# A capped attention with a token-mixing feed-forward layer on one Trainium2 core: the first load in one piece, the cap behind it, and fewer, larger products of zeros at the start

## The chip, the core and the metric

The kernel runs on one core of a Trainium2 chip. The metric is the device time of one execution in microseconds; the time of a kernel is the median of its runs. A profiled execution is a run of its own, with its own time.

## What is computed

The inputs are q, k and v for 4 batches of 12 heads, 448 tokens and a head dimension of 64, all in fp32, and four matrices of a feed-forward layer. In short:

```
scores = q k^T / 8                      (per batch and head, 448 x 448)
scores = cap * tanh(scores / cap)       (cap is an input, 30.0)
attn   = softmax(scores);  x = attn v   (heads side by side: 448 x 768 per batch)
h      = (x^T U V)^T                    (mixing over tokens, rank 32)
u      = x + h
out    = u + relu(u w_ch1) w_ch2        (768 -> 3072 -> 768)
```

## The kernel before

All arrays are held transposed, with features on the partitions. Attention works on pairs of heads: one tile `qk` of 128 x 2 x 448 words (448 KB) holds q and k of two heads, 64 partitions each. `four` lays out the work of four such pairs: `scores` (L435) multiplies one block of 128 keys of both heads with all queries, one head on the lower 64 rows of the array and one on the upper; `tanh` (L440, on ScalarE) reads the scores from PSUM with the scale `qsc` = 1/(8 cap); `exp` (L450, on ScalarE) follows for two blocks at once with the scale `capt` = cap. `rest` (L464) and `full` (L476) multiply with v; `normalize` and `mixin` do the softmax division (its reciprocals go through DRAM and come back as `rb`, L539) and the token mixing. The feed-forward layer follows: `up_seven` (L765) and `down` (L823), whose weights are converted by VectorE and ScalarE during the attention.

No order of instructions is written out by hand. Every step is a task with estimated costs per engine, an extra delay `lat` for loads, a priority (a smaller number goes first) and a due time `begin` in ns, before which it is not ready. `simulate` plays the tasks through with these estimates and so fixes the order of instructions on each engine; `emit` writes them out in that order. On the chip each engine then works through its own list and waits where an operand isn't there. So an estimate or a due time moves nothing directly; it can change the order. The PSUM tile of a first block of a step and that of its second (`sc`, `sc2`) must both be free before the next two blocks begin. The plan puts a task on TensorE only when nothing of lower number is ready, and charges 210 ns where its `mode` differs from that of the task before.

Three places are touched by the change.

- `consts` (L302 to 314) runs ahead of everything: it issues the load of the cap on ScalarE's queue as 128 words of 4 bytes, fills the tile `ones`, and computes `qsc` on VectorE (L313, L314).
- `fill` (L357 to 369) puts 25 products of zeros on TensorE, each 64 rows by 128 columns with 192 columns of data. Each fp32 product appears in the trace as two matmul records. The first 9 are due from 1000 ns every 330 ns with the first priority of all, the other 16 from 4000 ns every 600 ns with the last priority.
- In `four` the first `qk` tile is loaded by two DMAs (L408): all of q with the first 128 keys (288 KB), and the other 320 keys (160 KB). All other `qk` and `vn` (v) tiles come in one DMA each. All go through SP's queue. The planner charges each `qk` load of the first four pairs 2 ns a column of SP's time, so 1792 for a whole tile.

Of the kernel before, what the change touches and what calls it, by code (L numbers as in the profile page):

```python
# [11 lines left out]
F32 = mybir.dt.float32  # L12
# [3 lines left out]
AF = mybir.ActivationFunctionType  # L16
ALU = mybir.AluOpType

B, H, S, D = 4, 12, 448, 64
# [13 lines left out]
EARLY = 5, 6, 3, 2, 7, 1, 4  # L33

ALONE = 12
FILL, FIRST = 25, 9

# [206 lines left out]
class Build(Plan):  # L246
# [54 lines left out]
    def consts(self):  # L301
        nc = self.nc  # L302
        pool = self.opened(self.cp)
        self.capt = pool.tile([128, 1], F32, name="capt")
        nc.scalar.dma_start(out=self.capt, in_=self.cap.broadcast_to((128, 1)))
        self.qsc = pool.tile([128, 1], F32, name="qsc")
        self.ident = pool.tile([128, 128], F32, name="ident")
        self.ones = pool.tile([128, 3, 32], F32, name="ones")
        nc.vector.memset(self.ones, 0.0)
        nc.vector.memset(self.ones[:, 0], 1.0)  # L310
        for i in range(2):
            nc.vector.memset(self.ones[64 * i:64 * i + 64, 1 + i], 1.0)
        nc.vector.reciprocal(self.qsc, self.capt)  # L313
        nc.vector.tensor_scalar(out=self.qsc, in0=self.qsc, scalar1=1.0 / D ** 0.5, scalar2=None, op0=ALU.mult)  # L314

# [37 lines left out]
    def fill(self):  # L353


        nc = self.nc
        z = self.buf("ta", [128, DM // 2], F32, self.wp)  # L357
        bank = self.psum("misc")

        def blank(e):  # L360
            e.memset(z.t, 0.0)

        def turn():
            nc.tensor.matmul(bank.t[:, :192], z.t[:64, :128], z.t[:64, 192:], start=True, stop=True)  # L364

        self.task({"POOL": 500}, blank, w=[(z, 0)], prio=-1000)
        for i in range(FILL):
            begin = 1000 + 330 * i if i < FIRST else 4000 + 600 * (i - FIRST)
            self.task({"PE": 330}, turn, r=[(z, 0)], w=[(bank, 0)], begin=begin, prio=-1000 if i < FIRST else 1000, mode="sc")

    def attention(self):
# [17 lines left out]
    def four(self, p):  # L389


        nc = self.nc
        pools = (self.ap, self.pre) if p < ALONE else (self.ap,)
        prios = [p + i // 2 * 2 - 100 for i in range(4)]
        qks, vns = [], []
        for i in range(4):
            b, q = divmod(p + i, NP)
            if i % 2 == 0:
                vn = self.buf("vn", [128, 7, 2, D], F32, self.ap)
                vns.append(vn)  # L400
            qk = self.buf("qk", [128, 2, S], F32, *pools)
            qks.append(qk)

            cuts = (0, S + 128, 2 * S) if p + i == 0 else (0, 2 * S)
            for n, (lo, hi) in enumerate(zip(cuts, cuts[1:])):

                def load(b=b, q=q, qk=qk, lo=lo, hi=hi):
                    nc.sync.dma_start(  # L408
                        out=qk.t.rearrange("p a s -> p (a s)")[:, lo:hi],
                        in_=self.qk[b, q].rearrange("p a s -> p (a s)")[:, lo:hi])  # L410

                self.task({"SP": 2 * (hi - lo) if p == 0 else 350}, load,
                    w=[(qk, n), *([(qk, 1)] if len(cuts) == 2 else [])], lat=2600 if p == 0 else 4200, prio=prios[i])
            if i % 2:
                self.task({"SP": 350}, lambda b=b, q=q, vn=vn: nc.sync.dma_start(out=vn.t, in_=self.v[b, q // 2]),
                    w=[(vn, 0)], lat=4000, prio=prios[i], begin=6000 if p == 0 else 0)
# [3 lines left out]
        for g in range(7):  # L420
            th = self.buf("th", [128, 2, 2, S], F32, *pools)
            pss = [self.psum("sc", 2), self.psum("sc2", 2)]
            prio = prios[steps[2 * g][0]]
            for j in range(2):
                i, t = steps[2 * g + j]
                where[i, t] = th, j
                ps = pss[j]
                cs = (i - 1, i) if t == 3 else (i,)

                def scores(i=i, t=t, ps=ps, cs=cs):  # L430
                    for c in cs:
                        out = slice(64 * (c % 2), 64 * (c % 2) + 64) if t == 3 else slice(0, 128)
                        for a in range(2):
                            hd = slice(64 * a, 64 * a + 64)
                            nc.tensor.matmul(  # L435
                                ps.t[out, a, :S], qks[c].t[hd, 1, 128 * t:min(S, 128 * t + 128)], qks[c].t[hd, 0],
                                start=True, stop=True)

                def tanh(j=j, ps=ps, th=th):
                    nc.scalar.activation(out=th.t[:, j], in_=ps.t[:, :, :S], func=AF.Tanh, scale=self.qsc)  # L440

                r = [(qks[c], k) for c in cs for k in range(1 + (t > 0))]
                if j == 0:
                    self.task({"PE": 750}, scores, r=r, w=[(ps, 0), (pss[1], "next")], prio=prio, mode="q" if t == 3 else "sc")
                else:
                    self.task({"PE": 750}, scores, r=[*r, (pss[1], "next")], w=[(ps, 0)], prio=-300, mode="q" if t == 3 else "sc")
                self.task({"ACT": 920}, tanh, r=[(ps, 0)], w=[(th, j)], prio=prio)

            def exp(th=th):
                nc.scalar.activation(out=th.t, in_=th.t, func=AF.Exp, scale=self.capt)  # L450

            ks = [(th, 0), (th, 1)]
            self.task({"ACT": 1790}, exp, r=ks, w=ks, prio=prio)

        for h in range(2):
            vn, prio, i0 = vns[h], prios[2 * h], 2 * h
# [11 lines left out]
            for i, o in enumerate(os):  # L468
# [12 lines left out]
                def add(e, in0, in1, out):  # L481
# [5 lines left out]
                    prio=prio, lock=True)  # L487
                self.task({"DVE": 1090}, partial(add, in0=whole, in1=at(ts[2]), out=whole), r=ts[2:], w=[(es, 0)],
                    prio=prio, lock=True)
                if p < ALONE:  # L490
# [3 lines left out]
                        r=[(rth, rj)], w=[(es, 0)], prio=prio, lock=True)  # L494
                b, q = divmod(p + i0 + i, NP)
                u = self.u_bufs[b]
                self.task({"DVE": 620, "ACT": 560}, lambda e, q=q, o=o, u=u: self.copy(e, u.t[:, q], o.t[:, :S]), r=[(o, 0)],
                    w=[(u, q)], prio=prio)
# [405 lines left out]
```

## Time and profile before

| | us |
|---|---|
| three runs | 894.3, 893.38, 893.54 |
| median | 893.54 |
| the profiled execution | 890.19 |
| its span, from the first to the last instruction | 888.4 |
| TensorE busy in it | 874.8 (98%) |
| ScalarE busy | 447.1 (50%) |
| VectorE busy | 656.0 (74%) |
| first tanh of scores starts at | 8.88 |

Engines in the profile: PE is TensorE's matmul, PEld its weight loads, DVE VectorE, ACT ScalarE, POOL GpSimd, SP SyncE; a q behind the name is the engine's sequencer or its DMA issues. A group line gives engine, operation, output<-input, shapes, count and durations. The profile's rows of granted clock (PEclk) begin with the first recorded change; what the clock was before is to be read from the durations of like instructions.

### The profile page before, as it was taken

What the parts mean: (1) busy time and instruction counts of PE and PEld (TensorE: products, weight loads), DVE (VectorE), ACT (ScalarE), POOL (GpSimd) and SP (SyncE); (2) the same over time, 40 slices, a digit from 0 to 9 for tenths busy, and PEclk for the clock granted to TensorE, in tenths of its full rate; (3) what the DMA queues carried; (4) which work ended last, traced back from release to release, by engine and by line L of the source; (5) the groups of instructions that cost most, each with busy time, mean ns of one, the idle gap of its engine ahead of it and who ended that gap; (6) DMA issues with size and microseconds to landing.
All of it is one profiled execution on the core that took longest, in us unless ns stands there. A gap on an engine that the chain in (4) does not pass through costs nothing.

```text
span 888.4 us, 11752 instructions
## 1 busy us (share of the span) xinstructions
PE 874.8 (98%) x4418; PEld 701.3 (79%) x4418; DVE 656.0 (74%) x1116; ACT 447.1 (50%) x649; POOL 91.8 (10%) x125
## 2 busy tenths in 40 slices
PE   9999999998999999999999999999999999999998
PEld 6334343345899999998999999999999999999997
DVE  2688888858887777876877898776777766777644
ACT  5989898986554454554565455332223221232210
POOL 0111111110122111121121112000000000000000
PEclk9999999998999999999999999999999999999999
DMA  5653444412578887878978647521212212122003
GB/s 195 222 185 100 125 141 150 135 45 67 145 207 253 236 233 210 217 210 250 265 205 223 182 96 197 189 71 36 63 45 72 72 36 72 38 69 72 1 1 124
DMA packets 42424, 121.13 MB, mean 136 GB/s; under 512 B 5728, under 2 KB 18432, under 8 KB 42368
## 3 DMA queue, kind: packets, MB, share of 16 engines
q1 hardware_dynamic: 23024, 79.29, 28.0%
q0 software_dynamic: 12288, 22.22, 13.3%
q10 hardware_dynamic: 7056, 18.88, 5.4%
q8 instruction: 34, 0.56, 0.2%
q14 instruction: 22, 0.18, 0.1%
HBM read 79.28 MB, written 24.47 MB: 117 GB/s over the span
## 4 chain that ended last, share of the span: by engine, by line
PE 67%; issue 18%; POOL 4%; DVE 4%; ACT 3%; DMA 3%; POOLq 0%; ACTq 0%; DVEq 0%
PE mm L823 29%; PE mm L765 25%; PE sc L435 4%; PE o L476 4%; POOL u L836 4%; ACT th L440 2%; DMA rb<-rd 1%; PE misc L364 1%; PE misc L582 1%; DMA u<-st 1%; PE o L464 1%; ACT th L450 1%; PE misc L566 1%; DMA rd<-r 1%; DVE es L482 1%
## 5 line engine op out<-in xcount | busy, mean ns | idle before, releaser
L823 PE MATMUL mm<-g,w 128*128 128x448 f32 x1728 | 374.9, 366 | 1.3 <-ACT st L239 0.7
L823 PEld LDWEIGHTS mm<-g,w 128*128 128x128 f32 x1728 | 324.1, 188 | 30.9 <-ACT st L239 1.9
L765 PE MATMUL mm<-x,ws 128*128 128x448 f32 x1512 | 334.8, 369 | 2.8 <-DVE x L639 1.4
L765 PEld LDWEIGHTS mm<-x,ws 128*128 128x128 f32 x1512 | 285.3, 189 | 28.9 <-DVE x L639 1.7
L828 DVE TENSOR_TENSOR u<-u,mm 128x448 f32<-128x448 f32 x216 | 134.0, 621 | 58.2 <-PE mm L823 50.8
L239 ACT ACTIVATE cx<-mm 128x448 f32<-128x448 f32 x72 | 39.1, 545 | 118.4 <-PE mm L765 107.0
L836 POOL DMA_DIRECT2D u<-st x72 | 62.5, 868 | 265.7 <-ACT st L239 254.1
L778 DVE TENSOR_TENSOR cx<-cx,mm 128x448 f32<-128x448 f32 x72 | 44.6, 620 | 57.4 <-PE mm L765 56.8
L440 ACT ACTIVATE th<-sc,qsc 128x896 f32<-128x896 f32 x84 | 80.4, 1003 | 9.6 <-PE sc L435 9.5
L239 ACT ACTIVATE st<-mm 128x448 f32<-128x448 f32 x72 | 39.3, 546 | 86.5 <-PE mm L823 56.8
L435 PE MATMUL sc<-qk 64*128 64x448 f32 (+1 forms) x384 | 79.3, 574 | 0.6 <-ACT th L440 0.4
L450 ACT ACTIVATE th<-th,capt 128x1792 f32<-128x1792 f32 x42 | 75.3, 1793 | 1.1
L239 ACT ACTIVATE ws<-wa 128x384 fp32r<-128x384 f32 x53 | 27.2, 521 | 81.3 <-PE mm L765 81.2
L239 ACT ACTIVATE g<-cx 128x448 fp32r<-128x448 f32 x72 | 41.6, 578 | 42.6 <-DVE cx L778 40.3
L476 PE MATMUL o<-th,vn 128*64 128x448 f32 x288 | 60.2, 554 | 0.0
L639 DVE TENSOR_TENSOR ws<-ta,ws 128x384 fp32r<-128x384 f32 x96 | 53.0, 553 | 4.2 <-ACT ws L239 3.7
L292 DVE SCALAR_TENSOR_TENSOR wa<-wa,wr 128x768 int32<-128x768 int32 (+2 forms) x50 | 46.7, 935 | 11.8 <-ACT wa L284 11.0
L435 PEld LDWEIGHTS sc<-qk 64*128 64x128 f32 (+1 forms) x384 | 29.0, 175 | 31.5 <-issue 15.4
L482 DVE TENSOR_TENSOR es<-es,th 128x896 f32<-128x896 f32 (+1 forms) x36 | 39.1, 1086 | 13.8 <-ACT th L450 13.3
L695 DVE TENSOR_TENSOR w<-wa,w 128x768 fp32r<-128x768 f32 x48 | 45.7, 954 | 4.3 <-ACT w L239 4.1
L239 ACT ACTIVATE ws<-ta 128x384 fp32r<-128x384 f32 x58 | 30.2, 522 | 35.4 <-PE mm L765 32.2
L476 PEld LDWEIGHTS o<-th,vn 128*64 128x64 f32 x288 | 18.8, 138 | 36.6 <-issue 34.5
(67 smaller groups left out, 636.3 us busy)
## 6 DMA issues: line engine op xcount, KB each, us to landing
wr<-in_w SPq DMA_DIRECT2D x48, 768.0 KB, 5.6
kept<-wa ACTq DMA_DIRECT2D x48, 384.0 KB, 5.8
wa<-kept SPq DMA_DIRECT2D x48, 384.0 KB, 3.2
u<-st POOLq DMA_DIRECT2D x72, 224.0 KB, 5.3
qk<-in_qk SPq DMA_DIRECT2D x23, 448.0 KB, 3.8
vn<-in_v SPq DMA_DIRECT2D x12, 448.0 KB, 3.3
rb<-rd POOLq DMA_DIRECT2D x24, 224.0 KB, 3.7
out_t<-u SPq DMA_DIRECT2D x24, 224.0 KB, 2.9
```

Of the source, the lines that this page charges most:

```text
L239: e.activation(out=out, in_=in_, func=func)
L292: nc.vector.scalar_tensor_tensor(out=a_t().bitcast(I32), in0=a_t().bitcast(I32), scalar=3, in1=raw_t()[:, 0::2], op0=ALU.logical_shift_lef ...
L435: nc.tensor.matmul(ps.t[out, a, :S], qks[c].t[hd, 1, 128 * t:min(S, 128 * t + 128)], qks[c].t[hd, 0], start=True, stop=True)
L440: nc.scalar.activation(out=th.t[:, j], in_=ps.t[:, :, :S], func=AF.Tanh, scale=self.qsc)
L450: nc.scalar.activation(out=th.t, in_=th.t, func=AF.Exp, scale=self.capt)
L476: nc.tensor.matmul(o.t[64 * a:64 * a + 64, :S], vn.t[:, 3 * i + t, a], th.t[:, j, a], start=False, stop=t == 2)
L482: e.tensor_tensor(out=out(), in0=in0(), in1=in1(), op=ALU.add)
L639: e.tensor_tensor(out=lo, in0=src(), in1=hi.bitcast(F32), op=ALU.subtract)
L765: nc.tensor.matmul(ps.t[:, :S], ws[p].t[:, wi, sl], xs[p].t[:, xi, d], start=fresh and n == 0, stop=n == 8, skip_group_check=not fresh)
L823: nc.tensor.matmul(ps.t[:, :S], w1[f].t[:, wi, sl], g[b, f].t[:, gi], start=f == fs[0] and i == 0, stop=f == fs[-1] and i == 2)
L828: nc.vector.tensor_tensor(out=u.t[:, d], in0=u.t[:, d], in1=ps.t[:, :S], op=ALU.add)
L836: nc.gpsimd.dma_start(out=u.t[:, d], in_=st.t, accum_op=ALU.add)
```

## The change

The load of the cap moves from ScalarE's queue to SP's, right behind the first `qk` load, together with the two VectorE instructions that make `qsc` of it (`scales`). The first `qk` load becomes one DMA. ScalarE does a tanh of a column of `ones` at the beginning. The products of zeros use all 128 rows; there are 18 in place of 25, 5 of them first (due every 660 ns) and 13 from 7000 ns every 600 ns. The planner's estimate of a `qk` load of the first four pairs goes from 1792 ns (2600 later landed) to 900 ns (2900 later landed).

```diff
-FILL, FIRST = 25, 9
+FILL, FIRST = 18, 5
...
-        nc.scalar.dma_start(out=self.capt, in_=self.cap.broadcast_to((128, 1)))
...
+        warm = pool.tile([128, 1], F32, name="warm")
+        nc.scalar.activation(out=warm, in_=self.ones[:, 0, :1], func=AF.Tanh)
+
+    def scales(self):
+        nc = self.nc
+        nc.sync.dma_start(out=self.capt, in_=self.cap.broadcast_to((128, 1)))
         nc.vector.reciprocal(self.qsc, self.capt)
         nc.vector.tensor_scalar(out=self.qsc, in0=self.qsc, scalar1=1.0 / D ** 0.5, scalar2=None, op0=ALU.mult)
...
-            nc.tensor.matmul(bank.t[:, :192], z.t[:64, :128], z.t[:64, 192:], start=True, stop=True)
+            nc.tensor.matmul(bank.t[:, :192], z.t[:, :128], z.t[:, 192:], start=True, stop=True)
...
-            begin = 1000 + 330 * i if i < FIRST else 4000 + 600 * (i - FIRST)
+            begin = 1000 + 660 * i if i < FIRST else 7000 + 600 * (i - FIRST)
...
-            cuts = (0, S + 128, 2 * S) if p + i == 0 else (0, 2 * S)
-            for n, (lo, hi) in enumerate(zip(cuts, cuts[1:])):
-
-                def load(b=b, q=q, qk=qk, lo=lo, hi=hi):
-                    nc.sync.dma_start(
-                        out=qk.t.rearrange("p a s -> p (a s)")[:, lo:hi],
-                        in_=self.qk[b, q].rearrange("p a s -> p (a s)")[:, lo:hi])
-
-                self.task({"SP": 2 * (hi - lo) if p == 0 else 350}, load,
-                    w=[(qk, n), *([(qk, 1)] if len(cuts) == 2 else [])], lat=2600 if p == 0 else 4200, prio=prios[i])
+            def load(first=p + i == 0, b=b, q=q, qk=qk):
+                nc.sync.dma_start(out=qk.t, in_=self.qk[b, q])
+                if first:
+                    self.scales()
+
+            self.task({"SP": 900 if p == 0 else 350}, load, w=[(qk, 0)], lat=2900 if p == 0 else 4200, prio=prios[i])
...
-                r = [(qks[c], k) for c in cs for k in range(1 + (t > 0))]
+                r = [(qks[c], 0) for c in cs]
```

## Rows read from the trace of the kernel before

**Rows 1.** The page: the chain by engine; one kind of DMA issue with its median.
```profile
PE 67%; issue 18%; POOL 4%; DVE 4%; ACT 3%; DMA 3%; POOLq 0%; ACTq 0%; DVEq 0%
...
rb<-rd POOLq DMA_DIRECT2D x24, 224.0 KB, 3.7
```
**Rows 2.** The chain of waits, 0 to 40 us: start, length, what it was.
```profile
1.21 5.80 PE misc L364 x17
7.01 3.31 PE sc L435 x8
10.32 1.70 PE misc L364 x9
12.02 1.83 PE sc L435 x12
13.85 1.66 PE misc L364 x9
15.50 1.67 PE sc L435 x8
17.17 0.65 PE misc L364 x4
17.82 0.91 PE o L464 x8
18.73 2.40 PE o L476 x12
...
39.00 7.45 DMA rb<-rd
```
**Rows 3.** Timeline of ScalarE, first 16 us: start, length, [idle before <- releaser].
```profile
5.79 1.28 ACT L440 ACT_TABLE_LOAD   x1 [5.79 <-DVE qsc L314]
8.88 1.01 ACT L440 ACTIVATE th<-sc,qsc 128x896 f32<-128x896 f32 x1 [1.80 <-PE sc L435]
11.41 1.79 ACT L450 ACTIVATE th<-th,capt 128x1792 f32<-128x1792 f32 x1
15.03 1.79 ACT L450 ACTIVATE th<-th,capt 128x1792 f32<-128x1792 f32 x1
```
**Rows 4.** Zero products at 1.8 to 6.4, then 10.8 to 11.6; then scores, 6.9 to 10.2.
```profile
L364 PE MATMUL misc<-ta x16: 524/524/683, 1.2 to 6.2; 64*128 64x192 f32 x16
L364 PE MATMUL misc<-ta x7: 322/323/451, 10.4 to 11.5; 64*128 64x192 f32 x7
L435 PE MATMUL sc<-qk x8: 951/951/1112, 6.5 to 9.4; 64*128 64x448 f32 x8
```
**Rows 5.** DMA issues at 0.8 to 1.2, then at 22 to 23: KB, us to landing.
```profile
qk<-in_qk SPq DMA_DIRECT2D x1, 288.0 KB, 4.2
qk<-in_qk SPq DMA_DIRECT2D x1, 160.0 KB, 4.7
capt<-in_cap ACTq DMA_DIRECT2D x1, 0.5 KB, 4.6
...
qk<-in_qk SPq DMA_DIRECT2D x1, 448.0 KB, 3.1
```
**Rows 6.** One stretch; the last two columns are the DMA engines' busy share and GB/s.
```profile
2.00:4.00 2.00, 2.00 (x8) 2.00 (x8) 0.00 (x0) 0.00 (x0) 0.00 (x0) 1.00 0.66 127
```
**Rows 7.** Records of 448 columns at 60 to 100 us: 128 rows, then 64 rows.
```profile
L515 PE MATMUL misc<-es,ones x24: 539/551/563, 63.3 to 95.8; 128*32 128x448 f32 x24
L435 PE MATMUL sc<-qk x80: 536/536/640, 61.5 to 98.1; 64*128 64x448 f32 x64, 64*64 64x448 f32 x16
```
**Rows 8.** Two stretches in which TensorE starved; last columns: granted clock, DMA share, GB/s.
```profile
46.00:48.00 2.00, 0.31 (x3) 0.31 (x4) 1.46 (x2) 1.75 (x2) 0.20 (x1) 1.00 0.91 347
214.00:216.00 2.00, 0.47 (x1) 0.19 (x1) 2.00 (x5) 2.00 (x5) 0.00 (x0) 0.87 0.00 0
```
**Rows 9.** The chain of waits again, 34 to 110 us.
```profile
48.34 1.70 PE o L464 x8
50.04 3.21 PE o L476 x12
```

## The prediction

> **What bounds the kernel now.** I read the chain of waits by engine first, then the same chain in order of time. TensorE holds most of it [rows 1], so a microsecond that TensorE's list begins earlier is kept, unless something that doesn't move comes in between. The chain's first pieces are the place of the change [rows 2]: nine products of zeros (18 records, of which 17 are merged in the row) hold TensorE from 1.21 to 7.01, then come the first two blocks of scores up to 10.32, then five more zero products. The reader is to see that nothing but zeros stands on the chain until 7.01, although the first part of q/k had landed at 0.74 + 4.2 = 4.9 [rows 5]. ScalarE's timeline shows what waits: its table load from 5.79 to 7.07, idle 1.80 behind it for the scores, the first tanh at 8.88, the first exp at 11.41, the second at 15.03 [rows 3].
>
> The durations show the clock. A zero product takes 524 ns from 1.2 until past 6.2 and 323 from about 10.7 on; the first score records take 951, later ones 536 [rows 4, 7]. So up to some 10.5 us TensorE ran at 1.2 GHz, and at 2.4 after. It had been busy without a gap since 1.21, with products on 64 rows; the clock rose only after the first scores, which use both halves of the array.
>
> **The change part by part.** *Fewer zeros first.* Ten records stand ahead of the first scores instead of 18. The plan keeps that order, by its own estimates (used for the order alone): the fifth is due at 3640 and ends at 3970, the q/k tile is ready at 900 + 2900 = 3800, so the scores come sixth. At the low clock a record costs between 5.80/17 = 0.34 and (6.2 - 1.2)/15 = 0.33 [rows 2, 4], so 8 fewer are 2.6 us, and TensorE would be free for scores at 7.0 - 2.6 = 4.4. No row shows a zero product on 128 rows. The bounds are a 128-row and a 64-row record of 448 columns, 539 to 551 and 536 ns [rows 7]: rows cost next to nothing, 3% at most of 3.2 us, 0.1. I take 0.
>
> *The load.* In one piece it must land by 4.4. Alone on the DMA engines, a load of 448 KB takes 3.1 us from issue to landing [rows 5], so 0.74 + 3.1 = 3.85 is the early bound. The late bound is the second part of before, issued some 0.4 behind the first: 0.74 + 0.4 + 4.7 = 5.85. Between 2 and 4 us the DMA engines were busy 0.66 of the time for only 127 GB/s [rows 6], beside the cap's 128 words of 4 bytes, which landed at 0.74 + 4.6 = 5.3 from the other queue. With the cap behind it on the same queue, the load is nearest to the lone one; I take 4.1 (the first packets of a run may be late), which TensorE doesn't feel. At 5.85 the gain would fall by 1.45.
>
> *The cap* now lands behind 448 KB. VectorE's two instructions let ScalarE go 0.45 after its landing (5.79 - 5.34) [rows 3, 5]; VectorE has only these queued ahead of the first sum of exponentials, whose input is made after them anyway. The first tanh has its scores at 8.88 - 2.6 = 6.3, so the cap may land until 5.85. Early bound: with the load, 4.1. Late bound: its whole 4.6 counted from the load's landing, 8.7. I take 5.3, as before, since 16 engines then have 8 small words each and no rival. It costs nothing, with half a microsecond in hand. A page of the Trainium skill speaks against this move: by "DMA: Bandwidth & Descriptors" (Queues, rings and completion order), each engine takes descriptors in ring order, and a completion count lands only after every earlier write of that engine. By that the cap can't report before the whole q/k load has landed, where before it had its own ring. No run so far shows it; what it does here is a rival below.
>
> *The tanh of ones* brings the 1.28 us table load [rows 3] to the beginning, where ScalarE idles until 5.79. It saves nothing of before (1.80 idle stood behind the load), but without it the table would be ready at 5.75 + 1.28 = 7.0, 0.7 too late.
>
> *Queues.* SP issues as many DMAs ahead of the second q/k tile as before (the cap in place of the second part); ScalarE issues one less. The fifth q/k tile goes ahead of v in the new plan (SP is free at 3600, v is due at 6000). v is first used at 17.82 [rows 2], and all these loads are over by some 12. POOL's list stays.
>
> *The later zeros.* In the old plan five products follow the first two blocks, five the next two, two the next; the trace shows just these (records are halves) [rows 2]. By the new due times none fits the first gap, six go into the second, one into the third. Count from the start of the first exp, when both score tiles are free. Before: 12.02 - 11.41 = 0.61 of leftover zeros, 1.83 scores, 1.66 zeros, 1.67 scores, 0.65 zeros, so `rest` begins at 6.41. After: 1.83 + 1.98 + 1.67 + 0.33 = 5.81; the exp that `rest` needs ends at 15.03 + 1.79 - 11.41 = 5.41. So `rest` begins 0.6 sooner, and TensorE's chain with it [rows 2, 3]. If the old blocking stays, 0.
>
> *The clock.* If it doesn't rise before the second block of scores is done, the first exp comes at 11.41 - 2.6 = 8.8. If it is up when the first scores begin, tanh waits for the cap: two tanh of 1.01 from 5.75 give an exp at 7.8, 1.0 sooner. Full-array zeros followed by scores are what it rose after, so it should come some time within the scores; I take 0.3 of 0 to 1.0.
>
> Sum: 2.6 + 0.6 + 0.3 = 3.5 us. The profiled execution was 890.19 (span 888.4 and 1.8 around it) and would be 886.7. The median of the runs is 893.54, 3.35 above it, so I carry the gain over to that: 890.0.
>
> **Rivals.** *The clock rises during the zeros.* For it: full-array products with no gap. Against: 5.8 us of half-array zeros did nothing. The gain is 2.6 + 0.6 + 1.0 = 4.2: 889.3.
>
> *The cap becomes the bound*, behind 448 KB in one queue and with 128 reads of one word. At the late bound of 8.7 `qsc` is ready at 9.15, two tanh follow, the exp starts at 11.2: gain 0.2, and 0.6 later, so 892.7. It decides from a landing of 5.85, and in full only near 8.7. Against it: before, those words took less than that even in competition. The page named above points to this rival.
>
> *The gain doesn't arrive.* The two stretches in which TensorE starves, at 46 and 214 [rows 8], lie behind a read of `rb` [rows 2] and behind VectorE, busy 2.00 of 2.0 in the second. If these don't move with the start, 893.5. Against: their inputs are made by the same chain.
>
> *Slower: a new order.* Due times of 15000 and 20000 ns (the mixing constants, the first weights) stay, while the plan's attention moves up by 210 to 420 ns, so tasks after some 20 us of plan can change places. The place with a price is the `rb` read: 7.45 us on the chain among weight and q/k loads [rows 2], median 3.7 [rows 1]. TensorE starved for it (0.31 busy of 2.0), and afterwards ran at the low clock [rows 8]: `rest` 1.70 instead of 0.91, `full` 3.21 instead of 2.40 [rows 2, 9]. One more such collision costs 3.75 + 1.6 = 5.35: 895.4. It decides from a stall of 5.3, where 3.5 of gain and 1.8 are used up.
>
> *The falls go.* With the start moved, the starved stretches can lie otherwise against the clock's changes. The fall at 48 costs 1.6, that at 215 (0.47 busy of 2.0, then low) perhaps twice that; without the first 888.4, without both 885.
>
> **How the numbers follow.** The forecast, 890.0, has 0.42 (its own range 888.5 to 891.8); the early clock 0.13; the cap 0.10; no arrival 0.12; a new order 0.17; falls that go 0.06. A median of this kernel tells 0.2%, 1.8 us, from no change: faster is below 891.75. Faster: 0.39 of the forecast's 0.42, 0.13 and 0.06, together 0.58. Same: 0.03, the cap's 0.10, 0.10 of no arrival, together 0.23. Slower: 0.17 and 0.02, together 0.19. The range 887.0 to 895.5 leaves out the loss of both falls and the worse half of the new orders.
>
> **What would show it.** Right: the first scores' record near 4.4, the first tanh at 6.3 or sooner released by PE and not by `qsc`, the first exp at 8.8 or sooner, zeros falling from 524 to 323 ns before 8, `rest` 5.8 after the first exp. Wrong: TensorE idle for q/k after the tenth zero record; ScalarE released by VectorE; the same start but the first feed-forward products (L765) not 3.5 sooner.

## The result

| | before | changed |
|---|---|---|
| runs | 894.3, 893.38, 893.54, 894.15 | 884.61, 884.68, 881.73, 881.28 |
| median | 893.85 | 883.17 |
| the profiled execution | 890.19 | 884.61 |
| its span | 888.4 | 882.8 |

The ratio is 0.988 (95% interval 0.9854 to 0.9905). Two later measurements, each beside other runs of the kernel before, gave 884.87 against 892.25 (0.9926, 0.9901 to 0.995) and 884.2 against 892.13 (0.99, 0.9871 to 0.993). By these ratios the change brings 6.6 to 10.7 us; forecast were 3.5, and the measured time lies below the range. The profiled executions differ by 5.6. One run in a slower state (901.09, of before_tile2 below) is left out of the ratios.

The chain of waits of the changed kernel, first 60 us (start, length, what), answers to [rows 2, 9]:

```profile
1.21 3.57 PE misc L369 x10
4.77 3.02 PE sc L436 x8
...
7.82 1.02 ACT th L441
...
8.86 1.79 ACT th L451
...
14.31 0.98 PE o L465 x8
...
35.47 7.82 DMA rb<-rd
...
45.33 1.70 PE o L465 x8
47.04 3.05 PE o L477 x12
```

Ten zero records stand where 18 stood, scores begin at 4.77 instead of 7.01, the first exp at 8.86 instead of 11.41, `rest` (L465) at 14.31 instead of 17.82. The read of `rb` is as long as before, and the products behind it again run at the low clock. ScalarE's timeline and the zeros, against [rows 3, 4]:

```profile
0.73 1.28 ACT L313 ACT_TABLE_LOAD   x1 [0.73 <-PEq L894]
...
6.75 2.08 ACT L441 ACTIVATE th<-sc,qsc 128x896 f32<-128x896 f32 x2 [4.52 <-DVE qsc L319]
```
```profile
L369 PE MATMUL misc<-ta x10: 527/528/687, 1.2 to 4.2; 128*128 128x192 f32 x10
...
L369 PE MATMUL misc<-ta x12: 326/326/430, 9.8 to 11.7; 128*128 128x192 f32 x12
```

The first tanh was let go by `qsc`, not by the scores. A 128-row zero takes 528 ns at 1.2 GHz and 326 at 2.4, 3 to 4 ns more than one of 64 rows. The loads, against [rows 5]:

```profile
qk<-in_qk SPq DMA_DIRECT2D x1, 448.0 KB, 3.1
...
capt<-in_cap SPq DMA_DIRECT2D x1, 0.5 KB, 5.1
```

The whole first load landed at 0.74 + 3.1 = 3.8, the cap, issued at 1.18, at 6.3. The feed-forward part begins (first L766 product) at 203.32, in the kernel before (first L765 product) at 206.49: 3.2 us are made by then. The other 2.4 of the profiled pair come later, spread over the feed-forward part, and belong to something else (last section).

### The profile page after: what moved, and what is told of

It reads as the page before. It is cut to its first block, busy times and chain, and to the rows that moved or that the text cites. A ratio compares the mean times of both kernels' runs of the same rounds, so it can differ in the third digit from the quotient of the medians.

```text
span 882.8 us, 11722 instructions
## 1 busy us (share of the span) xinstructions
PE 868.7 (98%) x4404; PEld 695.6 (79%) x4404; DVE 656.1 (74%) x1116; ACT 447.4 (51%) x650; POOL 91.6 (10%) x125
## 4 chain that ended last, share of the span: by engine, by line
PE 53%; issue 29%; POOL 7%; DVE 4%; ACT 4%; DMA 3%; POOLq 0%; ACTq 0%; DVEq 0%
PE mm L824 21%; PE mm L766 18%; POOL u L837 7%; PE o L477 4%; PE sc L436 4%; ACT th L441 2%; ACT th L451 1%; DMA rb<-rd 1%; PE misc L583 1%; PE o L465 1%; DMA rd<-r 1%; PE misc L567 1%; DVE es L483 1%; DMA u<-st 1%; DVE x L640 1%
## 5 line engine op out<-in xcount | busy, mean ns | idle before, releaser
L766 PE MATMUL mm<-x,ws 128*128 128x448 f32 x1512 | 333.1, 368 | 3.4 <-DVE x L640 1.4
L766 PEld LDWEIGHTS mm<-x,ws 128*128 128x128 f32 x1512 | 285.1, 189 | 28.0 <-DVE x L640 1.7
L436 PEld LDWEIGHTS sc<-qk 64*128 64x128 f32 (+1 forms) x384 | 27.1, 175 | 33.7 <-issue 17.7
```

The lines of the kernel that those rows point to most:

```text
L436: nc.tensor.matmul(ps.t[out, a, :S], qks[c].t[hd, 1, 128 * t:min(S, 128 * t + 128)], qks[c].t[hd, 0], start=True, stop=True)
L766: nc.tensor.matmul(ps.t[:, :S], ws[p].t[:, wi, sl], xs[p].t[:, xi, d], start=fresh and n == 0, stop=n == 8, skip_group_check=not fresh)
```

## The experiments

Each kernel is the one before or the changed one with one or two edits. All ratios are against runs of the kernel before on the same chip. A ratio is not that of the two medians beside it: for later_only, first_only and fewer_only the medians differ by 1.5, 2.2 and 6.4 us, where the ratios give 2.5, 2.3 and 7.0.

| kernel | median | before beside it | ratio, 95% interval |
|---|---|---|---|
| before_again | 892.73 | 892.25 | 1.0004 (0.9985 to 1.0022) |
| after_again | 884.87 | 892.25 | 0.9926 (0.9901 to 0.995) |
| full_only | 890.84 | 892.25 | 0.9991 (0.9973 to 1.0009) |
| half_zeros | 885.45 | 892.25 | 0.9919 (0.989 to 0.9948) |
| after_no_tile | 884.49 | 892.64 | 0.9907 (0.9873 to 0.9941) |
| before_tile | 893.2 | 892.64 | 0.9988 (0.9961 to 1.0015) |
| after_two_tiles | 886.81 | 892.64 | 0.9938 (0.9911 to 0.9966) |
| fewer_only | 886.28 | 892.64 | 0.9922 (0.9894 to 0.995) |
| first_only | 887.8 | 890.04 | 0.9974 (0.9945 to 1.0002) |
| later_only | 888.54 | 890.04 | 0.9972 (0.9941 to 1.0004) |
| four_first | 884.41 | 890.04 | 0.993 (0.9903 to 0.9957) |
| after_look3 | 884.2 | 892.13 | 0.99 (0.9871 to 0.993) |
| before_tile2 | 891.16 | 892.13 | 0.9991 (0.9965 to 1.0018) |
| no_later | 886.78 | 892.13 | 0.9927 (0.9902 to 0.9951) |
| double_half | 895.31 | 891.51 | 1.0043 (1.0008 to 1.0079) |
| double_full | 895.2 | 891.51 | 1.0038 (1.0015 to 1.0061) |

### The same kernels once more

> The kernel before once more, unchanged. The profiled executions differ by 5.6 us (890.2 and 884.6), 3.2 of them made by 205 us into the span, but the medians differ by 10.7. Theory (clock): in most executions of the kernel before, TensorE's clock rises later than in the profiled one or falls more often, since 64-row zeros don't lift it; the executions listed with their granted clock should show less of the full clock than 0.994, and a profiled one that takes about 894 should show zero products of 524 ns beyond 10.7 us or more low stretches. Rival (rate): all of TensorE's products run some 0.3% slower in it than in the changed kernel, with the same clock; then the granted clock is 0.994 to 0.997 and the difference grows evenly from 205 to 885 us.

The profiled execution took 894.92. Its chain of waits up to 26 us:

```profile
7.01 3.31 PE sc L435 x8
10.32 2.88 PE misc L364 x9
13.20 3.51 PE sc L435 x12
16.71 3.17 PE misc L364 x9
19.89 2.64 PE sc L435 x8
22.53 0.65 PE misc L364 x4
23.18 0.91 PE o L464 x8
```

This is the program of [rows 2], unchanged, and up to 10.32 it has the same times. There the five zeros of the first gap take 2.88 instead of 1.70, the next scores 3.51 instead of 1.83, the next five zeros 3.17 instead of 1.66: TensorE ran at 1.2 GHz until about 21.7, and `rest` begins at 23.18 instead of 17.82, 5.4 us later. At that clock zeros and scores take 6.4 to 6.7 us per step, where ScalarE needs 3.6, so TensorE is the bound and the zeros are pure delay. The clock theory holds for the start of this execution; that it would show less of the full clock later on did not come (0.998). The three other profiles of the kernel before have the rise at 9.5 to 10.7 and `rest` at 17.1 to 17.8. Two of them were taken to see how often the rise is late: for the last of them about one execution in two had been expected to rise beyond 12 us, and the rival, 8 to 11 us again, came in both. So the late rise is seen in one of four profiles.

> The changed kernel once more, unchanged: 881 to 885, first exp of scores at 8.9, clock up at 4.6 to 8. Under the clock theory its executions differ by whole low stretches (1.7 us each); under the rate rival they agree within 0.5 us.

Its first exp starts at 8.19, 0.67 sooner than in the first profile of the changed kernel: the clock was up at 4.3, within the zeros, and the first tanh went at 6.26, straight after `qsc`.

### Rows of the zeros alone

```diff
-            nc.tensor.matmul(bank.t[:, :192], z.t[:64, :128], z.t[:64, 192:], start=True, stop=True)
+            nc.tensor.matmul(bank.t[:, :192], z.t[:, :128], z.t[:, 192:], start=True, stop=True)
```

(in the kernel before: full_only; the other way round in the changed kernel: half_zeros)

> The kernel before with its 25 zero products on 128 rows in place of 64, nothing else. Clock theory: the clock is up before 8 us, the last of the 9 first zeros or the first scores run at 2.4 GHz, the first exp comes 1 to 2 us sooner than 11.4, and the executions lose what they lose to a late clock: 886 to 889. Rival (rate, or the load, or the number of zeros): 893 to 894, or 1 us below at most.

> The changed kernel with its 18 zero products on 64 rows, as before the change. Clock theory: the clock rises only after the first scores and in some executions later still, 886 to 890, that is 4 or more slower than the changed kernel. Rival (it is the load, the cap and the fewer zeros): within 1 us of the changed kernel, 882 to 884.

Both misses. The rows do move the clock: in the profiles with 128-row zeros at the start its first recorded change is a rise at 4.3 to 7.4 (nine profiles), with 64-row zeros at 8.5 to 10.7 (ten) and once at 21.7. In full_only the last first zeros already run at 326 ns and the first exp starts at 9.68:

```profile
9.68 1.79 ACT L450 ACTIVATE th<-th,capt 128x1792 f32<-128x1792 f32 x1
```
```profile
6.67 1.77 PE L435 MATMUL sc<-qk 64*128 64x448 f32 x8
8.38 1.89 PE L364 MATMUL misc<-ta 128*128 128x192 f32 x10
10.20 1.94 PE L435 MATMUL sc<-qk 64*128 64x448 f32 x12
12.07 1.89 PE L364 MATMUL misc<-ta 128*128 128x192 f32 x10
13.89 1.77 PE L435 MATMUL sc<-qk 64*128 64x448 f32 x8
15.59 0.92 PE L364 MATMUL misc<-ta 128*128 128x192 f32 x4
16.44 0.98 PE L464 MATMUL o<-th,vn 64*64 64x448 f32 x8
```

This is its TensorE timeline: no gap from 6.67 to 16.44, even at the high clock. The twelve zeros of the gaps (24 records) hold TensorE, so of 1.73 us at the first exp 1.3 are left at `rest` (9.68 and 16.44 against 11.41 and, in the same view, 17.75). Its runs still spread from 888.78 to 894.97. What it gains at the start it can lose later: its runs have a mean granted clock of 0.9942, those of the kernel before beside it 0.9953. Over the span that is 1 us more of full clock lost to later falls. In half_zeros the first exp starts at 8.86, just as in the changed kernel. So 128 rows by themselves bring nothing that these runs can tell.

### The number of zeros

```diff
-FILL, FIRST = 25, 9
+FILL, FIRST = 18, 5
...
-            begin = 1000 + 330 * i if i < FIRST else 4000 + 600 * (i - FIRST)
+            begin = 1000 + 660 * i if i < FIRST else 7000 + 600 * (i - FIRST)
```

(both lines in the kernel before: fewer_only; with 21, 5, the first ones due every 660 ns and the later ones from 4000 as before: first_only; with 22, 9 and the later ones from 7000: later_only)

> The kernel before with the new number and due times of the zeros alone (5 and 13, still on 64 rows; load in two parts, cap on the other queue, no tanh at the beginning). By the first steps of the forecast: scores wait for the first part of the load until 5.0, the first tanh for the table load until 7.1, the first exp starts at 9.2 to 9.4 (8.9 in the changed kernel, 11.4 before), `rest` 5.8 behind it instead of 6.4, and the rate is 203.9: 889 to 890. Rival (the load and the cap are what counts): above 891.

> The kernel before with 5 instead of 9 zeros ahead of the first scores, the 16 others as before (64 rows, five of them between the second and the third block of scores). Theory (late clock): this gives the 2.1 to 2.6 us of the start; but the five zeros of the first gap stay and at the low clock take 3.2 us between the scores, so the clock still rises late in a part of the executions: 889.5 to 890.5. Rival (the number of zeros ahead of the scores decides all of it): 886 to 887, as with both edits.

> The kernel before with 9 zeros ahead as before and 13 later ones from 7000 ns in place of 16 from 4000; one instead of five then stands in the first gap between scores. Late-clock theory: four blocks of scores follow each other almost without zeros, the clock is up soon after the first scores in every execution: first exp at 11.4 at the latest, `rest` 0.6 sooner, and the executions with a late clock are gone: 888 to 889.5. Rival: only the 0.6 to 0.9, 891 to 892.

first_only brings 890.04 x 0.0026 = 2.3 us, later_only 2.5, both together 892.64 x 0.0078 = 7.0. By themselves they are at the edge of what the runs tell (both intervals reach 1), so neither can be priced; together they are clear, and the sum of 4.8 agrees with the 7.0 within its error. With both, scores wait for the first part of the load, and the chain is that of the forecast:

```profile
0.74 4.09 DMA qk<-in_qk
...
4.88 3.38 PE sc L435 x8
...
9.32 1.79 ACT th L450
...
14.78 0.98 PE o L464 x8
```

`rest` comes 5.46 after the first exp. In later_only the first exp is where it was, and `rest` 0.9 sooner (16.86 against 17.75 in the same view):

```profile
16.86 0.98 PE L464 MATMUL o<-th,vn 64*64 64x448 f32 x8 [0.15 <-ACT th L450]
```

It waits for ScalarE there and no longer for zeros. What the profile doesn't show is the spread: ten runs of later_only lie between 887.16 and 889.84, 25 of the kernel before beside them between 886.87 and 898.86. The lowest are alike; the long ones are gone. With first_only, which keeps the five zeros of the first gap, ten runs lie between 885.72 and 891.89.

### Larger zeros

```diff
-        def turn():
-            nc.tensor.matmul(bank.t[:, :192], z.t[:64, :128], z.t[:64, 192:], start=True, stop=True)
+        def turn(k):
+            for _ in range(k):
+                nc.tensor.matmul(bank.t[:, :192], z.t[:64, :128], z.t[:64, 192:], start=True, stop=True)
...
+            self.task({"PE": 330}, partial(turn, 1 if i < FIRST else 2), r=[(z, 0)], w=[(bank, 0)], begin=begin, prio=-1000 if i < FIRST else 1000, mode="sc")
```

(double_half; double_full is the same with all 128 rows)

> The kernel before with each of the 16 later zeros doubled (two products each, 64 rows); the first 9 as before. Late-clock theory: ten 64-row products then stand in each of the first two gaps between scores, 6.4 us each at the low clock, so the clock rises after 20 us in most executions: 3 to 8 us slower than the kernel before, 895 to 900. Rival (the zeros between scores matter only by their time in the gaps): at the high clock ten take 3.3 us where the gap has about 2.1, so 1.5 to 2.5 us slower, 894.

> The same with all zeros on 128 rows. Late-clock theory: the clock is up by 8 us and stays, so only the time in the gaps is paid, 1.5 to 2.5 us less the 1.3 that the early clock brought in the kernel with 25 single 128-row zeros: 891 to 893, and 4 or more below the 64-row twin. Rival (rows don't matter): the same as the 64-row twin within 1 us.

The medians are alike, so the rows bring nothing here either: the rival of double_full came, the late-clock theory did not. The time of double_half, 3.8 us above the kernel before, lies in the range of its theory, but not by the theory's mechanism. In its profile the clock was up at 10.5, and `rest` began 3.8 later than the 17.82 of [rows 2]:

```profile
13.54 1.83 PE sc L436 x12
15.36 3.28 PE misc L365 x19
...
21.61 0.91 PE o L465 x8
```

That is the rival's cost, the time of the zeros in the gaps, which had been put at 1.5 to 2.5. Ten 64-row zeros in a gap did not hold the clock down in this execution. The chain of double_full, in which the clock was up at 5.2:

```profile
6.32 1.70 PE sc L436 x8
8.03 3.45 PE misc L365 x20
11.47 1.86 PE sc L436 x12
13.34 3.45 PE misc L365 x20
16.79 1.70 PE sc L436 x8
18.49 1.50 PE misc L365 x8
19.99 0.91 PE o L465 x8
```

A step of scores and zeros takes 5.2 us with 3.6 of ScalarE's work beside it: zeros between scores cost their whole length once TensorE has no slack. Only the spread differs: 892.27 to 904.29 with 64 rows (one execution; the next longest is 897.3), 892.71 to 896.17 with 128.

### A place 32 bytes further on

The tile `warm` moves the tiles allocated behind it by 32 bytes. In after_no_tile the first tanh writes into `qsc`'s tile instead; before_tile and after_two_tiles have an unused tile more:

```diff
-        warm = pool.tile([128, 1], F32, name="warm")
-        nc.scalar.activation(out=warm, in_=self.ones[:, 0, :1], func=AF.Tanh)
+        nc.scalar.activation(out=self.qsc, in_=self.ones[:, 0, :1], func=AF.Tanh)
```
```diff
+        self.pad = pool.tile([128, 1], F32, name="pad")
```

> The changed kernel with the first tanh written into qsc's tile, so that no tile `warm` is allocated and all tiles behind it lie 32 bytes lower, as before the change. Theory (place): the feed-forward products run at 203.0 ns a record in the changed kernel and 203.9 in the one before because the new tile moves the tiles on the left by 32 bytes; here they run at 203.9 again, and with 3240 records the time is 2.8 us longer than the changed kernel's: 887.5 to 888. Rival (program): the rate comes from something else of the change, such as the number or kind of zeros; then 885 and 203.0 ns.

> The kernel before with one unused tile of 128 x 1 words behind `ones` and nothing else, so that the tiles behind it lie 32 bytes higher. Place theory: 203.0 ns a record in the feed-forward part, 2.8 us shorter than the kernel before: 889 to 890, with the start as before. Rival: 203.9 ns and 892.3.

> The changed kernel with a second unused tile, so that the tiles behind it lie 64 bytes higher than before the change instead of 32. If what counts is the place against steps of 64 bytes: 203.9 ns a record and 887.5 to 888. If it is any move, or the step is longer: 203.0 ns or another value, and 885.

> The kernel before with one unused tile of 128 x 1 words behind `ones`, once more. If the rate of the feed-forward products belongs to the kernel, 205 ns a record between 600 and 870 us as in the first look; if to the chip or the moment, the same as the changed kernel's on this chip.

> The changed kernel once more, beside before_tile2 on the same chip. Late-clock theory: no execution lies more than 4 us above the lowest, those of the kernel before spread over 7 and more; difference of the means 6 to 7 us. Rate: if it belongs to the chip, both kernels have 203.0 or both about 205 ns a record.

By the times, the tile does nothing: 0.9907 without it beside 0.988 to 0.9926 with it; 0.9988 and 0.9991 for the kernel before with it. The place theory falls as a cause of the gain. On the chip that before_tile2 and after_look3 share, the rates were 203.0 and 205.1, so they belong neither to the kernel nor to the chip alone; the last section has them. In after_look3 the difference of the means is 7.7, and its runs lie up to 5.8 us above the lowest, where at most 4 had been expected.

### Fewer still

```diff
-FILL, FIRST = 18, 5
+FILL, FIRST = 17, 4
```

(four_first; no_later has 4, 4. Both write the first tanh into `qsc`'s tile.)

> The changed kernel with 4 instead of 5 zeros ahead of the first scores, and the first tanh written into qsc's tile so that no further tile is allocated. The load lands at 3.84, four zeros end at 4.1 to 4.2, five at 4.7: the first scores begin 0.6 sooner, the first tanh waits for the cap (6.28) or comes just with it, the first exp is up to 0.6 sooner: 884.0 to 884.6 where the changed kernel has 884.9. If the cap is the bound, no gain: 884.9.

> The changed kernel with 4 zeros ahead of the first scores and none later, and no further tile. If the scores alone keep the clock up: `rest` begins right behind the second exp, 5.5 after the first exp instead of 5.5 to 5.8, and 0 to 0.4 us less than with the 13 later zeros: 884.0. If the later zeros are needed: the clock falls between 10 and 25 us in some executions, each fall 1 to 4 us, and the mean lies above 885.

Neither beats the changed kernel by anything that these runs tell. In four_first the cap is the bound, the case for which no gain had been expected:

```profile
1.16 4.87 DMA capt<-in_cap
...
6.58 1.02 ACT th L440
```

In no_later `rest` follows 5.46 after the first exp (13.77 and 8.31), and no fall is recorded between 10 and 25 us in its profile. Its six runs lie between 885.4 and 888.19, above the 884.0 of the one case and with the mean above 885 of the other; whether the later zeros are worth something stays open.

## Why the prediction was wrong

**Step by step the profiled execution came close, in part by luck.** *Fewer zeros first*: scores began 2.24 us sooner (7.01 to 4.77), forecast 2.6. *The clock*: up at 7.4 in the profiled execution, at 4.3 and 6.0 in the two others, forecast "within the scores". The reason given there, that it rose after full-array zeros and scores, was in no row: the kernel before has none on 128 rows. Zeros and clock together moved the first exp by 2.55, forecast 2.9. *Later zeros*: `rest` came 5.45 after the first exp, forecast 5.8, before 6.4. The forecast counted all scores of the first gap behind the first exp; the trace has the first of them at 7.81, behind the first tanh, and then `rest` waited for ScalarE. So one term was 0.35 too large and the other 0.36 too small, and that `rest` began 3.5 sooner, as forecast, is luck.

*The load*: 3.8 us, forecast 4.1; it isn't on the chain. *The cap*: it landed at 6.3, where I took 5.3 and had hand until 5.85. So it held the first tanh until 6.75, which cost nothing on the chain here, since the second tanh waited for scores until 7.82. With the clock up early it is the bound (after_again, four_first). By the Trainium skill ("DMA: Bandwidth & Descriptors", Queues, rings and completion order) a completion count lands only after every earlier write of the same DMA engine. The trace agrees as far as that goes: the cap came 2.5 us after the load that it was put behind. The Trainium skill says this engine by engine; that the whole load must land first is the prediction's own step, and why the cap came 2.5 us later and not at once no run shows. *The tanh of ones*: 1.28 us of table load taken off the start, as forecast. At the feed-forward part the gain was 3.2; 3.5 had been forecast.

**The step that failed is the last of the sum**: "The median of the runs is 893.54, 3.35 above it, so I carry the gain over to that". It takes every execution to gain what the profiled one does, so that the zeros, the terms 2.6 and 0.6, would be worth 3.2 in the runs too. fewer_only, the new zeros alone, measures 7.0 (4.5 to 9.5), and the whole change 6.6 to 10.7 in its three measurements. The 3.35 were no constant either. The changed kernel has no such gap: its profiled execution (884.61) lies above the median of its runs. The kernel before, run again, spreads over 7 to 12 us on each chip.

**So the mis-sized term is the zeros**, first and later together: 3.2 by their length in one profile, 7.0 measured. How the 7.0 divide between the two is not shown (first_only 2.3, later_only 2.5, each with an interval that reaches 0). Load, cap and tanh move the first exp by another 0.46 (9.32 to 8.86) and can't be told from nothing in the times.

**What the profile did not show.** Two things are on record. One is a late rise of the clock: before_again stays at 1.2 GHz over the first three steps and loses 5.4 us to it. That the zeros between the scores, being on half of the array, hold the clock down there is argued; double_half, with twice as many, speaks against it. The other is later falls. The mean granted clock of each run, which counts the time before the first rise as full, averages 0.9957 in the 109 runs of the kernel before that stand beside the experiments, and 0.9975 in the 54 further runs of the seven kernels with four or five zeros first and the others from 7000. By span that is 3.9 us of full clock lost against 2.2, so up to 1.7 us of the gain, by estimate, are fewer falls. They weigh on the times: of the 109, the 37 with 0.997 or more average 889.8 us, the 37 with 0.994 or less 893.7. Why the falls became fewer was not tested.

**Of the rivals**, the early clock did occur in two of the changed kernel's three profiles and brought the first exp 0.67 and 0.50 sooner, not 1.0; in after_again the cap then holds the tanh. The cap as the bound occurred with it, at a fraction of its price: the first tanh went at 6.26, where the rival had `qsc` ready at 9.15. The new order did not occur: apart from the zeros, TensorE's list is the same in both programs. The falls that go occurred in one profile of three (after_look3 has neither fall), and in part in the mean of the runs, as above.

**What stays open.** That late rises make up the rest of the gain is shown in one execution and argued for the others, from the spread. later_only has the granted clock of the kernel before beside it (0.9965 both), so its narrow spread is not a matter of later falls; that it is late rises that went is not shown by a profile. Other executions are long for other reasons: the profiled one of before_tile lost 5.4 us on the first profile of the kernel before between 140 and 150 us, where a read of `rb` took 6.53 us in place of 3.94 and the clock fell behind it.

## What to carry to other kernels

A profile is one execution: where it lies below the runs by more than they differ among themselves, look for what it was spared, read the granted clock of every run, and profile again before carrying a sum over to the median. Filler work on an engine can have the price of its length at the engine's lowest clock (here 5.4 us in one execution). Put it ahead of the first real work, where the engine waits for a load anyway, and not between steps that have no slack at that clock.

## What had not been expected of the hardware

The feed-forward products run at other rates when the tiles lie 32 or 64 bytes further on. TensorE's records between 600 and 870 us, fully busy at the granted clock 1.00, in before_again, then in the changed kernel's first profile, its third (after_look3), and before_tile2 (the column behind the window's length is busy time and number of matmul records):

```profile
600.00:870.00 270.00, 270.00 (x1327) 248.70 (x1326) 186.43 (x331) 70.27 (x122) 0.00 (x0) 1.00 0.17 50
```
```profile
600.00:870.00 270.00, 270.00 (x1331) 249.76 (x1331) 186.17 (x329) 70.72 (x122) 0.00 (x0) 1.00 0.16 49
```
```profile
600.00:870.00 270.00, 270.00 (x1318) 247.11 (x1317) 184.53 (x326) 69.60 (x120) 0.00 (x0) 1.00 0.16 49
```
```profile
600.00:870.00 270.00, 270.00 (x1332) 249.77 (x1331) 186.36 (x329) 70.72 (x122) 0.00 (x0) 1.00 0.16 49
```

Start to start that is 203.9, 203.0, 205.1 and 203.0 ns a record. All kernels with the old places have 203.9 in every profile (13, on at least five chips); in the seven profiles with the tiles moved it is 203.0 or 205.0 to 205.1, and one and the same program has 203.0 in one execution and 205.1 in another. The 2.4 us that the first profiled pair gains late fit this: 0.9 ns over some 3300 records is about 3 us by estimate. They are luck. What sets the rate was not found.
